# Fewer DMA issues on SyncE, a new allowance in the scheduler, and the last output tile in column halves

## The chip, the cores and the metric

The kernel runs on one core of one Trainium2 chip. The metric is the time of one execution on the device, in microseconds (us). The kernel before took 228.57 us (median of 4 runs, 227.63 to 229.99). A profile shows one execution, its span from the first to the last instruction.

## The reference, cut to what matters

```python
xn = layernorm(x)                                   # x: 2048 x 512
kv = shift_conv(k, shift_k) * v
y  = irfft(rfft(pad(kv)) * rfft(pad(ssm_k)))[:S]    # long convolution, length 4096
s  = xn * (y + kv * ssm_D)
g  = silu(w_down @ (gelu(xn @ w_gate) * (xn @ w_up)))   # 512 -> 1792 -> 512
return x + s * g
```

The Fourier transforms are done as matmuls in two stages each, with the data written to HBM and read back between the stages (ZH, ZK, ZS, ZI), because that rearranges it. The feed-forward part is TensorE's filler: plain matmuls that wait for nothing late.

## The kernel before

A small scheduler inside the program orders some hundreds of tasks before anything is built: each has an engine, an estimated duration and a priority, and the order in which it picks them becomes the fixed program of each engine. Each engine then goes through its own program in that order, with semaphore waits. So a matmul that stands too early in TensorE's program stops everything behind it: the first one that reads BK did so for 3.52 us.

```python
# scheduler: earliest start of a task after its dependency d
base = max(base, d.end + d.lat + (self.HEDGE if d.nbytes and t.opts[0][0] == "PE" else self.SEM))   # HEDGE = 1500 ns
...
# one quarter of XN transposed into xnT: four DMAs on SyncE
for j in range(4):
    S.add([("SP", 350.0)], f_transpose(j), ...)
...
# filter spectrum n read back, rows 0..127 and the two halves swapped: three DMAs
dma(e, HS[:, j, 0, :, :], ZS[n], ...)
for h in range(2):
    dma(e, HS[64 * h:64 * h + 64, j, 1, :, :], ZS[n, 64 - 64 * h:128 - 64 * h], ...)
...
# inverse result stored
S.add([("SP", 350.0)], st, r=[bo], w=[bZ["I"][n]], prio=0, nbytes=262144)
...
# end, for each pair of tiles
G = (tanh + 1) * psum ; XN = y_psum * XN ; G = G * XN ; G = G + X ; write out (256 KB)
```

Names used below: BH and BK are the inputs of the second stage for the filter and for the data; HB is the product of the two spectra (VectorE); BO is the inverse's result, copied from PSUM by ScalarE into one of two buffers and stored as ZI; BI reads it back. HS is a filter spectrum, read back from ZS; xnT is XN transposed.

## Time and profile before

| | before |
|---|---|
| median time | 228.57 us |
| profiled execution | 231.43 us, span 229.6 us |
| TensorE busy | 209.8 us (91%) |
| first matmul of real work, end of TensorE | 14.82, 224.33 us |
| after TensorE's end | 5.3 us |

In profile lines PE is TensorE (PEld its weight loads), DVE VectorE, ACT ScalarE and POOL GpSimd; SPq and ACTq are DMAs issued by SyncE and ScalarE; "out<-in" names what is written and what is read. A clock of 1.00 is TensorE at full speed, and psall is PSUM, where TensorE's results stand.

The prediction shows where TensorE waits. Here is the end of the program, on ScalarE and VectorE (start, duration, instruction, in brackets the idle time before it and what ended it):

```profile
224.35 0.60 ACT L1055 ACTIVATE G<-psall 128x512 bf16<-128x512 f32 x1 [1.56 <-PE psall L575]
224.98 0.69 DVE L1057 SCALAR_TENSOR_TENSOR G<-G,psall 128x512 bf16<-128x512 bf16 x1 [1.47 <-ACT G L1055]
225.71 0.69 DVE L1101 TENSOR_TENSOR G<-G,XN 128x1024 bf16<-128x1024 bf16 x1
226.43 0.69 DVE L1103 TENSOR_TENSOR G<-G,X 128x1024 bf16<-128x1024 bf16 x1
```

Four dependent steps follow the last matmul, then the write of two tiles.

### The profile page before, as it was taken

What the parts mean: (1) busy time and instruction counts of PE and PEld (TensorE: products, weight loads), DVE (VectorE), ACT (ScalarE), POOL (GpSimd) and SP (SyncE); (2) the same over time, 40 slices, a digit from 0 to 9 for tenths busy, and PEclk for the clock granted to TensorE, in tenths of its full rate; (3) what the DMA queues carried; (4) which work ended last, traced back from release to release, by engine and by line L of the source; (5) the groups of instructions that cost most, each with busy time, mean ns of one, the idle gap of its engine ahead of it and who ended that gap; (6) DMA issues with size and microseconds to landing.
All of it is one profiled execution on the core that took longest, in us unless ns stands there. A gap on an engine that the chain in (4) does not pass through costs nothing.

```text
span 229.6 us, 2869 instructions
## 1 busy us (share of the span) xinstructions
PE 209.8 (91%) x970; PEld 94.6 (41%) x988; DVE 169.3 (74%) x252; ACT 118.6 (52%) x151; POOL 17.5 (8%) x42
## 2 busy tenths in 40 slices
PE   7788999999959999999939999969899999999990
PEld 2553444444414444444413444424344444444440
DVE  5995799689973989892228599869677447999543
ACT  4498886767726977993620553442464332133121
POOL 8634000013000000001000000000000000000000
PEclk9999999999997999999985999999999999999998
DMA  6999999989798688789788999999951277712311
GB/s 192 385 348 359 392 373 390 416 328 189 172 320 272 237 254 275 260 283 328 196 264 283 246 285 277 325 304 316 299 189 60 91 240 254 240 46 93 141 46 46
DMA packets 47759, 57.48 MB, mean 250 GB/s; under 512 B 13824, under 2 KB 32001, under 8 KB 47744
## 3 DMA queue, kind: packets, MB, share of 16 engines
q1 hardware_dynamic: 44864, 51.00, 70.6%
q10 hardware_dynamic: 2880, 6.29, 8.1%
q8 instruction: 8, 0.13, 0.2%
q14 instruction: 7, 0.06, 0.1%
HBM read 35.78 MB, written 18.87 MB: 238 GB/s over the span
## 4 chain that ended last, share of the span: by engine, by line
PE 35%; issue 22%; SPq 18%; DMA 16%; DVE 4%; ACT 2%; POOL 1%; POOLq 0%; ACTq 0%
PE psall L575 35%; SPq L552 16%; DMA ZI<-BO 8%; DMA X<-in_A_q_dram 6%; DMA BK<-ZK 2%; SPq L773 2%; ACT BO L571 1%; DVE XN L761 1%; DVE stats L749 1%; POOL mv L758 1%; DVE HT L1040 1%; POOLq L381 0%; DVE G L1101 0%; DVE G L1057 0%; DVE G L1103 0%
## 5 line engine op out<-in xcount | busy, mean ns | idle before, releaser
L575 PE MATMUL psall<-xnT,Wg 128*128 128x512 bf16 x224 | 56.5, 389 | 0.7 <-ACT BO L571 0.4
L575 PE MATMUL psall<-xnT,Wu 128*128 128x512 bf16 x224 | 56.3, 384 | 0.1
L1037 ACT ACTIVATE GE<-psall 128x512 bf16<-128x512 f32 x56 | 33.0, 597 | 44.8 <-PE psall L575 43.5
L575 PE MATMUL psall<-Wd,HT 128*128 128x512 bf16 x219 | 51.3, 379 | 0.2
L1040 DVE TENSOR_TENSOR HT<-psall,GE 128x512 bf16<-128x512 f32 x56 | 37.6, 685 | 14.0 <-PE psall L575 12.2
L1003 DVE TENSOR_TENSOR HB<-psall,HS 128x1024 bf16<-128x1024 f32 x32 | 37.1, 1218 | 14.2 <-PE psall L575 14.2
L575 PEld LDWEIGHTS psall<-xnT,Wg 128*128 128x128 bf16 x224 | 22.2, 100 | 29.3 <-issue 3.1
L575 PEld LDWEIGHTS psall<-xnT,Wu 128*128 128x128 bf16 x224 | 22.0, 99 | 27.8 <-issue 1.6
L575 PEld LDWEIGHTS psall<-Wd,HT 128*128 128x128 bf16 x224 | 22.0, 98 | 26.4
L571 ACT ACTIVATE BO<-psall 128x1024 bf16<-128x1024 f32 x16 | 16.4, 1024 | 22.0 <-DMA ZI<-BO 12.3
L1057 DVE SCALAR_TENSOR_TENSOR G<-G,psall 128x512 bf16<-128x512 bf16 x16 | 10.7, 684 | 18.6 <-ACT G L1055 18.6
L1055 ACT ACTIVATE G<-psall 128x512 bf16<-128x512 f32 x16 | 9.3, 598 | 19.3 <-PE psall L575 19.2
L571 ACT ACTIVATE ASH<-psall 128x1024 bf16<-128x1024 f32 x16 | 16.3, 1021 | 2.7 <-PE psall L575 2.3
L575 PE MATMUL psall<-HB,MT 128*128 128x512 bf16 x61 | 15.8, 379 | 0.8 <-ACT BO L571 0.6
L938 DVE TENSOR_TENSOR KAC<-KAC,KTM 128x2048 bf16<-128x2048 bf16 x12 | 14.6, 1220 | 0.2
L936 DVE TENSOR_TENSOR KTM<-KK,SKB 128x2048 bf16<-128x2048 bf16 x12 | 14.6, 1217 | 0.1
L575 PE MATMUL psall<-BK,MT 128*128 128x512 bf16 x30 | 9.3, 412 | 5.2 <-DMA BK<-ZK 3.5
L749 DVE BATCH_NORM_STATS2 stats<-X 128x6 f32<-128x512 bf16 x16 | 10.4, 675 | 4.3 <-DMA X<-in_A_q_dram 4.3
L965 ACT ACTIVATE AST<-psall 128x1024 bf16<-128x1024 f32 x11 | 11.1, 1025 | 2.6 <-PE psall L575 2.6
L575 PE MATMUL psall<-BH,MT 128*128 128x512 bf16 x30 | 9.5, 408 | 2.8 <-DVE KTM L936 2.0
L758 POOL TENSOR_TENSOR mv<-mv,NHALF 128x4 f32<-128x4 f32 (+1 forms) x5 | 5.4, 1084 | 78.9 <-DVE mv L757 78.9
L1090 DVE TENSOR_TENSOR XN<-psall,XN 128x1024 bf16<-128x1024 f32 x8 | 9.6, 1216 | 0.7 <-PE psall L575 0.7
(69 smaller groups left out, 157.5 us busy)
## 6 DMA issues: line engine op xcount, KB each, us to landing
ZH<-ASH ACTq DMA_DIRECT2D x16, 256.0 KB, 5.8
BH<-ZH SPq DMA_DIRECT2D x16, 256.0 KB, 3.7
HS<-ZS SPq DMA_DIRECT2D x16, 256.0 KB, 5.7
HS<-ZS SPq DMA_DIRECT2D x32, 128.0 KB, 5.1
BK<-ZK SPq DMA_DIRECT2D x16, 256.0 KB, 5.6
ZI<-BO SPq DMA_DIRECT2D x16, 256.0 KB, 4.5
BI<-ZI SPq DMA_DIRECT2D x16, 256.0 KB, 4.3
ZS<-AST SPq DMA_DIRECT2D x11, 256.0 KB, 3.3
```

The source lines that it names most:

```text
L552: trk.dma(eng, lambda e: e.dma_start(out=out_ap, in_=in_ap), sem, r=r, w=w)
L571: return h.activation(o, i, ACTF.Copy)
L575: return h.matmul(o, lhsT=l, rhs=r, start=st, stop=sp)
L749: op([("DVE", 670.0)], lambda e, h, t=t: h.bn_stats(stats[:, t, :], X[:, t, :]), r=[bX[q][t % 4 // 2]], w=[bst[t]], rr=[R_X[t]], ww=[R_st[ ...
L936: op([("DVE", dur)], lambda e, h, j=j, m=m: h.tensor_tensor(KTM[:, m.slot, :, :], kk(j), sk(j), ALU.mult), r=need + [bSKB, a], w=[m], rr=l ...
L938: op([("DVE", dur)], lambda e, h, m=m: h.tensor_tensor(KAC[:, a.slot, :, :], KAC[:, a.slot, :, :], KTM[:, m.slot, :, :], ALU.add), r=[m], ...
L965: op([("ACT", act(1024))], lambda e, h, p=p, a=a: h.activation(ast["K"][a.slot].rearrange("p c d -> p (c d)"), ps(psl(p)), ACTF.Copy, scal ...
L1003: op([("DVE", dve(1024, 1))], lambda e, h, k=k, pk=pk, qq=qq, hs=hs: h.tensor_tensor(HB[:, qq.slot, :, :].rearrange("p c d -> p (c d)"), p ...
L1037: op([("ACT", act(512))], lambda e, h: h.activation(GE[:, g.slot, :], bank(pg), ACTF.Gelu_apprx_tanh), r=[pg], w=[g], rr=lambda: R_bank(pg ...
L1040: op([("DVE", dve(512, 1))], lambda e, h: h.tensor_tensor(HT[:, q % 2, m, :], bank(pu), GE[:, g.slot, :], ALU.mult), r=[pu, g], w=[bHT[q][m]],
L1057: op([("DVE", dve(512, 1))], lambda e, h, t=t, p=p: h.scalar_tensor_tensor(out=G[:, t, :], in0=G[:, t, :], scalar=1.0, in1=bank(p), op0=AL ...
L1090: op([("DVE", dve(1024, 1))], lambda e, h, p=p, xs=xs: h.tensor_tensor(xs, ps(psl(p)), xs, ALU.mult), r=[p], w=[bS[j], bXN[2 * j], bXN[2 * ...
```

## The change

The intent: relieve SyncE's in-order queue, let TensorE meet its DMA inputs later, and shorten the end. The core of the diff:

```diff
-    HEDGE = 1500.0
+    HEDGE = 3000.0          # 1000 for the first loads
...
-                for j in range(4):                      # four transposes per quarter
-                    ... in_=XN[:, 4 * q + j, :], transpose=True
-                    S.add([("SP", 350.0)], f, ...)
+                ... in_=XN[:, 4*q:4*q+4, :].rearrange("p t d -> p (t d)"), transpose=True
+                S.add([("SP", 2600.0)], f, ...)         # one, with a longer estimate
...
+                dma(e, ZS[n, 128:192], ast["K"][a.slot][0:64], ...)   # first half stored twice
-                three reads of HS
+                src = bass.AP(ZS, n * 192 * 2 * DM, [[2 * DM, 128], [128 * DM, 2], [1, 2 * DM]])
+                dma(e, HS[:, hs.slot], src, ...)                      # one read
...
-            S.add([("SP", 350.0)], ... BK read ..., prio=0.4)
+            S.add([("SP", ISSUE)], ... BK read ..., prio=-0.5)        # ISSUE = 470
-            S.add([("SP", 350.0)], st, ... ZI store ...)
+            S.add([("ACT", 350.0)], st, ... ZI store ..., lat=STORE)
-        one 1 MB transpose F1 -> G1, after stage 1
+        four of 256 KB, after the ninth inverse
...
+                cols = [(0, DM)] if t < NT - 1 else [(0, DM // 2), (DM // 2, DM)]
+                for c0, c1 in cols:
+                    g, rg = G[:, t, c0:c1], [R_G[t]]                  # region of the whole tile
+                    tanh -> g ; u = psum * XN ; g = (g + 1) * u ; g = g + x ; write out
```

Beside these, the second half of the first X load is issued by ScalarE, for the first six pairs of tiles G is multiplied by XN ahead of the inverse's last stage, and some of the scheduler's estimates change (470 ns instead of 350 for most DMA issues of SyncE, 800 instead of 1450 for one step of GpSimd).

More of the change, by code (lines that the diff above doesn't have):

```diff
@@ L27 @@
 STORE = 5000.0
+ISSUE = 470.0
 NC_PAIRS = 3
@@ L318, in run @@
                 for d in t.deps:
-                    base = max(base, d.end + d.lat + (self.HEDGE if d.nbytes and t.opts[0][0] == "PE" else self.SEM))
+                    base = max(base, d.end + d.lat + (self.SEM if not d.nbytes or t.opts[0][0] != "PE" else 1000.0 if d.eng.startswith("loads") else self.HEDGE))
                 ok = True
@@ L455, in build_kernel @@
         ZK = nc.dram_tensor("ZK", [NG, 128, DM], BF16, kind="Internal")
-        ZS = nc.dram_tensor("ZS", [NG // 2, 128, 2, DM], BF16, kind="Internal")
+        ZS = nc.dram_tensor("ZS", [NG // 2, 192, 2, DM], BF16, kind="Internal")
         ZI = nc.dram_tensor("ZI", [NG, 128, DM], BF16, kind="Internal")
@@ L523, in build_kernel @@
         R_BK = [res(f"BK{j}", BK[:, j, :, :]) for j in range(6)]
-        R_HS = [[res(f"HS{j}_0", HS[:, j, 0, :, :])] + [res(f"HS{j}_1{h}", HS[64 * h:64 * h + 64, j, 1, :, :]) for h in range(2)] for j in range(4)]
+        R_HS = [res(f"HS{j}", HS[:, j, :, :, :]) for j in range(4)]
         R_HB = [res(f"HB{j}", HB[:, j, :, :]) for j in range(6)]
@@ L530, in build_kernel @@
                "S": [trk.free_res(f"ZS{t}") for t in range(16)],
+               "D": [trk.free_res(f"ZD{t}") for t in range(16)],
                "I": [trk.free_res(f"ZI{t}") for t in range(16)]}
@@ L583, in build_kernel @@
         bmv = [[B(f"mv{q}_{h}") for h in range(2)] for q in range(NQ)]
-        bxnT = [[B(f"xnT{q}_{h}") for h in range(4 if q else 2)] for q in range(NQ)]
+        bxnT = [[B(f"xnT{q}_{h}") for h in range(1 if q else 2)] for q in range(NQ)]
         bF1, bG1, bMT, bid, bSKB = [B(f"F1_{i}") for i in range(4)], [B(f"G1_{i}") for i in range(4)], B("MT"), B("id"), B("SKB")
@@ L596, in build_kernel @@
         bG = [B(f"G{j}") for j in range(8)]
+        bGX = [B(f"GX{j}") for j in range(6)]
         bconst, bIO, bCC, bSKR = B("const"), [B(f"IO{i}") for i in range(4)], B("CC"), B("SKR")
@@ L706, in load_x @@
                 for h in range(2):
-                    load(f"x{q}_{h}", X[:, 2 * h:2 * h + 2, :], x_dr[:, 2 * h:2 * h + 2, :], R_X[2 * h:2 * h + 2], [bX[0][h]], 262144)
+                    load(f"x{q}_{h}", X[:, 2 * h:2 * h + 2, :], x_dr[:, 2 * h:2 * h + 2, :], R_X[2 * h:2 * h + 2], [bX[0][h]], 262144, ("SP", "ACT")[h])
         def load_w(i):
@@ L757, in ln @@
                 op([("DVE", 180.0)], lambda e, hd, ts=ts: hd.tensor_scalar(mv[:, ts, 2:3], mv[:, ts, 1:2], LN_EPS, None, ALU.add), r=bm, w=[be], rr=rm, ww=rm, prio=pr)
-                t_pw = op([("POOL", 1450.0)], lambda e, hd, ts=ts, n=n: hd.tensor_tensor(mv[:, ts, 3:4], mv[:, ts, 2:3], NHALF[:, 0:n, :], ALU.pow),
+                t_pw = op([("POOL", 800.0)], lambda e, hd, ts=ts, n=n: hd.tensor_tensor(mv[:, ts, 3:4], mv[:, ts, 2:3], NHALF[:, 0:n, :], ALU.pow),
                           r=[bconst, be] + bm, w=[b], rr=rm + [R_nh], ww=rm, prio=-2)
@@ L763, in ln @@
             return t_pw
-        d_xt = [dsem(f"d_xt{j}") for j in range(4)]
+        d_xt = dsem("d_xt")
         def xn_transpose(q):
@@ L769, in xn_transpose, with f @@
             if q:
-                for j in range(4):
-                    def f(e, j=j):
-                        o = xnT[:, q % 2, j, :, :]
-                        trk.dma(e, lambda h: h.dma_start(out=o, in_=XN[:, 4 * q + j, :], transpose=True), d_xt[j], r=[R_XN[4 * q + j]], w=[R_xnT[q % 2][j]])
-                    S.add([("SP", 350.0)], f, r=[bXN[4 * q + j]], w=[bxnT[q][j]], prio=-1, nbytes=131072, after=af)
+                def f(e):
+                    o = xnT[:, q % 2, :, :, :].rearrange("k j d p -> k (j d) p")
+                    trk.dma(e, lambda h: h.dma_start(out=o, in_=XN[:, 4 * q:4 * q + 4, :].rearrange("p t d -> p (t d)"), transpose=True), d_xt, r=R_XN[4 * q:4 * q + 4], w=R_xnT[q % 2])
+                S.add([("SP", 2600.0)], f, r=bXN[4 * q:4 * q + 4], w=bxnT[q], prio=-1, nbytes=524288, after=af)
                 return
@@ L790, in xn_transpose @@
                    rr=lambda p=p: R_bank(p), ww=R_xnT[q % 2][2 * hf:2 * hf + 2], prio=-1, after=af)
+        d_out = []
         gu_tasks = [[] for _ in range(NQ)]
@@ L901, in st @@
                 dma(e, dst, ast[x][a.slot], d_ast[x][a.slot], [R_AST[x][a.slot]], [R_Z[x][t]])
-            t_st = S.add([("ACT" if x == "H" else "SP", 350.0)], st, r=[a], w=[bZ[x][t]], prio=0, lat=STORE if x == "H" else 0.0, nbytes=262144 if x == "K" else 0)
+            t_st = S.add([("ACT", 350.0) if x == "H" else ("SP", ISSUE)], st, r=[a], w=[bZ[x][t]], prio=0, lat=STORE if x == "H" else 0.0, nbytes=262144 if x == "K" else 0)
             if x == "H":
@@ L957, in build_kernel @@
         d_bh = [dsem(f"d_bh{j}") for j in range(4)]
+        d_dup = [dsem(f"d_dup{j}") for j in range(5)]
         h2_tasks = []
@@ L961, in h_stage2 @@
             bh, p, a = B(f"bh{n}", pBH), B(f"psf{n}", pC), B(f"hf{n}", pAST["K"])
-            S.add([("SP", 350.0)], lambda e, n=n, bh=bh: dma(e, BH[:, bh.slot, :, :], z_pair(ZH, n), d_bh[bh.slot], R_Z["H"], [R_BH[bh.slot]]),
+            S.add([("SP", ISSUE)], lambda e, n=n, bh=bh: dma(e, BH[:, bh.slot, :, :], z_pair(ZH, n), d_bh[bh.slot], R_Z["H"], [R_BH[bh.slot]]),
                   r=bZ["H"], w=[bh], prio=0.5, nbytes=262144, after=zh_tasks)
@@ L966, in h_stage2, with st @@
                r=[p], w=[a], rr=lambda p=p: R_ps[psl(p)], ww=lambda a=a: [R_AST["K"][a.slot]], prio=2.5, after=kshift_tasks[:1])
-            S.add([("SP", 350.0)], lambda e, n=n, a=a: dma(e, ZS[n], ast["K"][a.slot], d_ast["K"][a.slot], [R_AST["K"][a.slot]], [R_Z["S"][n]]),
-                  r=[a], w=[bZ["S"][n]], prio=0, nbytes=262144)
+            def st(e, n=n, a=a):
+                dma(e, ZS[n, 0:128], ast["K"][a.slot], d_ast["K"][a.slot], [R_AST["K"][a.slot]], [R_Z["S"][n]])
+                dma(e, ZS[n, 128:192], ast["K"][a.slot][0:64], d_dup[a.slot], [R_AST["K"][a.slot]], [R_Z["D"][n]])
+            S.add([("SP", 950.0)], st, r=[a], w=[bZ["S"][n]], prio=0, nbytes=393216)
         for n in range(16):
@@ L974, in build_kernel @@
             stage1("K", t, V[:, t, :], R_V[t], [bKV[t // 4]], ZK, 3)
-        d_g1 = dsem("d_g1")
-        S.add([("SP", 350.0)], lambda e: trk.dma(e, lambda h: h.dma_start(out=G1[:].rearrange("k t c p -> k (t c) p"), in_=F1[:].rearrange("p t c k -> p (t c k)"), transpose=True),
-                                                d_g1, r=R_F1, w=R_G1), r=bF1, w=bG1, prio=8, nbytes=1048576, after=s1_tasks["K"])
         d_bk = [dsem(f"d_bk{j}") for j in range(6)]
-        d_hs = [[dsem(f"d_hs{j}_{h}") for h in range(3)] for j in range(4)]
+        d_hs = [dsem(f"d_hs{j}") for j in range(4)]
         d_bo = [dsem(f"d_bo{j}") for j in range(2)]
@@ L991, in ld_s @@
             def ld_s(e, n=n, hs=hs):
-                j = hs.slot
-                dma(e, HS[:, j, 0, :, :], ZS[n], d_hs[j][0], [R_Z["S"][n]], [R_HS[j][0]])
-                for h in range(2):
-                    dma(e, HS[64 * h:64 * h + 64, j, 1, :, :], ZS[n, 64 - 64 * h:128 - 64 * h], d_hs[j][1 + h], [R_Z["S"][n]], [R_HS[j][1 + h]])
-            S.add([("SP", 1000.0)], ld_s, r=[bZ["S"][n]], w=[hs], prio=0.5, nbytes=524288, after=kshift_tasks)
-            S.add([("SP", 350.0)], lambda e, n=n, bk=bk: dma(e, BK[:, bk.slot, :, :], z_pair(ZK, n), d_bk[bk.slot], R_Z["K"], [R_BK[bk.slot]]),
-                  r=bZ["K"], w=[bk], prio=0.4, nbytes=262144)
+                src = bass.AP(ZS, n * 192 * 2 * DM, [[2 * DM, 128], [128 * DM, 2], [1, 2 * DM]])
+                dma(e, HS[:, hs.slot, :, :, :].rearrange("p k c d -> p k (c d)"), src, d_hs[hs.slot], [R_Z["S"][n], R_Z["D"][n]], [R_HS[hs.slot]])
+            S.add([("SP", ISSUE)], ld_s, r=[bZ["S"][n]], w=[hs], prio=0.5, nbytes=524288, after=kshift_tasks)
+            S.add([("SP", ISSUE)], lambda e, n=n, bk=bk: dma(e, BK[:, bk.slot, :, :], z_pair(ZK, n), d_bk[bk.slot], R_Z["K"], [R_BK[bk.slot]]),
+                  r=bZ["K"], w=[bk], prio=-0.5, nbytes=262144)
             S.add([("PE", pe(2))], fwd(pk, BK, R_BK, bk), r=[bMT, bk], w=[pk], prio=3.5, lat=200.0, after=t_inv[n - 2:n - 1] if n >= 2 else [])
@@ L1004, in build_kernel @@
                     HB[:, qq.slot, :, :].rearrange("p c d -> p (c d)"), ps(psl(pk)), HS[:, hs.slot, k, :, :].rearrange("p c d -> p (c d)"), ALU.mult),
-                   r=[pk, hs], w=[qq], rr=lambda k=k, pk=pk, hs=hs: R_ps[psl(pk)] + (R_HS[hs.slot][1:] if k else R_HS[hs.slot][:1]), ww=lambda qq=qq: [R_HB[qq.slot]], prio=0.9)
+                   r=[pk, hs], w=[qq], rr=lambda k=k, pk=pk, hs=hs: R_ps[psl(pk)] + [R_HS[hs.slot]], ww=lambda qq=qq: [R_HB[qq.slot]], prio=0.9)
             def inv(e, pi=pi, q1=q1, q2=q2):
@@ L1013, in build_kernel @@
             t_inv.append(S.add([("PE", pe(4))], inv, r=[bMT, q1, q2], w=[pi], prio=3, lat=200.0))
-            op([("ACT", act(1024)), ("DVE", dve(1024, 1))], lambda e, h, pi=pi, bo=bo: copy(e, h, BO[:, bo.slot, :, :].rearrange("p c d -> p (c d)"), ps(psl(pi))),
+            op([("ACT", act(1024))], lambda e, h, pi=pi, bo=bo: copy(e, h, BO[:, bo.slot, :, :].rearrange("p c d -> p (c d)"), ps(psl(pi))),
                r=[pi], w=[bo], rr=lambda pi=pi: R_ps[psl(pi)], ww=lambda bo=bo: [R_BO[bo.slot]], prio=0.9)
@@ L1018, in st, with g1 @@
                 dma(e, bass.AP(ZI, 2 * n * 128 * DM, [[DM, 128], [128 * DM, 2], [1, DM]]), BO[:, bo.slot, :, :], d_bo[bo.slot], [R_BO[bo.slot]], [R_Z["I"][n]])
-            S.add([("SP", 350.0)], st, r=[bo], w=[bZ["I"][n]], prio=0, nbytes=262144)
+            S.add([("ACT", 350.0)], st, r=[bo], w=[bZ["I"][n]], prio=0.8, lat=STORE)
+        d_g1 = [dsem(f"d_g1{i}") for i in range(4)]
+        for i in range(4):
+            def g1(e, i=i):
+                ts = slice(4 * i, 4 * i + 4)
+                trk.dma(e, lambda h: h.dma_start(out=G1[:, ts].rearrange("k t c p -> k (t c) p"), in_=F1[:, ts].rearrange("p t c k -> p (t c k)"), transpose=True),
+                        d_g1[i], r=R_F1[ts], w=R_G1[ts])
+            S.add([("SP", 1350.0)], g1, r=[bF1[i]], w=[bG1[i]], prio=8, nbytes=262144, after=[t_inv[8]])
         def unit(q, m):
@@ L1044, in down @@
             for jt in range(4):
-                p = B(f"psd{q}_{jt}", pF)
                 t = 4 * q + jt
-                for m0, m1 in ((0, 4), (4, 9), (9, 14)):
-                    def f(e, p=p, jt=jt, m0=m0, m1=m1):
-                        for m in range(m0, m1):
-                            trk.op("PE", lambda h, m=m: mm(h, bank(p), HT[:, q % 2, m, 128 * jt:128 * (jt + 1)], Wd[:, m, :], m == 0, m == MF - 1),
-                                   r=[R_HT[q % 2][m], R_Wd[m // 7]], w=R_bank(p), accum=True)
-                    down_tasks[q].append(S.add([("PE", pe(m1 - m0))], f, r=(bHT[q] if jt else bHT[q][m0:m1]) + bWd[m0 // 7:(m1 + 6) // 7], w=[p], prio=9 + q - 0.5 if jt or m1 == MF else 10.05 + q, lat=200.0))
@@ L1054, in down @@
-                bt = B(f"tanh{q}_{jt}")
-                op([("ACT", act(512))], lambda e, h, t=t, p=p: h.activation(G[:, t, :], bank(p), ACTF.Tanh, scale=0.5), r=[p], w=[bt],
-                   rr=lambda p=p: R_bank(p), ww=[R_G[t]], prio=1, after=zh_tasks + (h2_tasks if q >= 2 else []))
-                op([("DVE", dve(512, 1))], lambda e, h, t=t, p=p: h.scalar_tensor_tensor(out=G[:, t, :], in0=G[:, t, :], scalar=1.0, in1=bank(p), op0=ALU.add, op1=ALU.mult),
-                   r=[p, bt], w=[bG[t // 2]], rr=lambda p=p, t=t: R_bank(p) + [R_G[t]], ww=[R_G[t]], prio=1)
+                cols = [(0, DM)] if t < NT - 1 else [(0, DM // 2), (DM // 2, DM)]
@@ new lines, in down, with pc, f @@
+                for c0, c1 in cols:
+                    p = B(f"psd{q}_{jt}_{c0}", pF)
+                    def pc(p=p, c0=c0, c1=c1):
+                        return bank(p)[:, c0:c1]
+                    for m0, m1 in ((0, 4), (4, 9), (9, 14)):
+                        def f(e, p=p, jt=jt, m0=m0, m1=m1, pc=pc, c0=c0, c1=c1):
+                            for m in range(m0, m1):
+                                trk.op("PE", lambda h, m=m: mm(h, pc(), HT[:, q % 2, m, 128 * jt:128 * (jt + 1)], Wd[:, m, c0:c1], m == 0, m == MF - 1),
+                                       r=[R_HT[q % 2][m], R_Wd[m // 7]], w=R_bank(p), accum=True)
+                        down_tasks[q].append(S.add([("PE", pe(m1 - m0, c1 - c0))], f, r=(bHT[q] if jt else bHT[q][m0:m1]) + bWd[m0 // 7:(m1 + 6) // 7],
+                                                   w=[p], prio=9 + q - 0.5 if jt or m1 == MF else 10.05 + q, lat=200.0))
+                    n = c1 - c0
+                    g, rg = G[:, t, c0:c1], [R_G[t]]
+                    bt = B(f"tanh{q}_{jt}")
+                    op([("ACT", act(n))], lambda e, h, g=g, pc=pc: h.activation(g, pc(), ACTF.Tanh, scale=0.5), r=[p], w=[bt],
+                       rr=lambda p=p: R_bank(p), ww=rg, prio=1, after=zh_tasks + (h2_tasks if q >= 2 else []))
+                    if q < NQ - 1:
+                        op([("DVE", dve(512, 1))], lambda e, h, g=g, pc=pc: h.scalar_tensor_tensor(out=g, in0=g, scalar=1.0, in1=pc(), op0=ALU.add, op1=ALU.mult),
+                           r=[p, bt], w=[bG[t // 2]], rr=lambda p=p, rg=rg: R_bank(p) + rg, ww=rg, prio=1)
+                        continue
+                    u, x = XN[:, t, c0:c1], X[:, t, c0:c1]
+                    bu, b2 = B(f"u{t}_{c0}"), B(f"o{t}_{c0}")
+                    op([("DVE", dve(n, 1))], lambda e, h, u=u, pc=pc: h.tensor_tensor(u, pc(), u, ALU.mult), r=[p, bS[t // 2]], w=[bu],
+                       rr=lambda p=p, t=t: R_bank(p) + [R_XN[t]], ww=[R_XN[t]], prio=0.8)
+                    op([("DVE", dve(n, 1))], lambda e, h, g=g, u=u: h.scalar_tensor_tensor(out=g, in0=g, scalar=1.0, in1=u, op0=ALU.add, op1=ALU.mult),
+                       r=[bu, bt], w=[b2], rr=rg + [R_XN[t]], ww=rg, prio=1)
+                    op([("DVE", dve(n, 2))], lambda e, h, g=g, x=x: h.tensor_tensor(g, g, x, ALU.add), r=[b2], w=[b2], rr=rg + [R_X[t]], ww=rg, prio=1)
+                    R_o, d_o = trk.free_res(f"outl{t}_{c0}"), dsem(f"d_outl{t}_{c0}")
+                    d_out.append(d_o)
+                    S.add([("SP", ISSUE)], lambda e, t=t, c0=c0, c1=c1, g=g, rg=rg, R_o=R_o, d_o=d_o: dma(e, out_dr[:, t, c0:c1], g, d_o, rg, [R_o]),
+                          r=[b2], w=[B(f"outl{t}")], prio=1, nbytes=256 * n)
@@ L1065, in build_kernel @@
                 unit(q, m)
-            down(q)
+            if q < NQ - 1:
+                down(q)
         d_bi = [dsem(f"d_bi{j}") for j in range(8)]
@@ L1079, in ld @@
                     dma(e, BI[:, bi.slot, :, :], src, d_bi[bi.slot], R_Z["I"], [R_BI[bi.slot]])
-                S.add([("SP", 350.0)], ld, r=bZ["I"], w=[bi], prio=0.5, nbytes=262144)
+                S.add([("SP", ISSUE)], ld, r=bZ["I"], w=[bi], prio=0.5, nbytes=262144)
             def y(e, j=j, bis=bis, p=p):
@@ L1088, in build_kernel @@
             S.add([("PE", pe(4))], y, r=[bG1[j // 2]] + bis, w=[p], prio=3, lat=200.0)
-            xs = XN[:, 2 * j:2 * j + 2, :].rearrange("p t d -> p (t d)")
-            op([("DVE", dve(1024, 1))], lambda e, h, p=p, xs=xs: h.tensor_tensor(xs, ps(psl(p)), xs, ALU.mult), r=[p], w=[bS[j], bXN[2 * j], bXN[2 * j + 1]],
-               rr=lambda p=p, j=j: R_ps[psl(p)] + R_XN[2 * j:2 * j + 2], ww=R_XN[2 * j:2 * j + 2], prio=3)
-        d_out = [dsem(f"d_out{j}") for j in range(8)]
-        for j in range(8):
+            ts = slice(2 * j, 2 * j + 2)
@@ new lines, in build_kernel @@
+            xs, g = (T[:, ts, :].rearrange("p t d -> p (t d)") for T in (XN, G))
+            if j < 6:
+                op([("DVE", dve(1024, 2))], lambda e, h, g=g, xs=xs: h.tensor_tensor(g, g, xs, ALU.mult), r=[bG[j], *bXN[ts]], w=[bGX[j]],
+                   rr=R_G[ts] + R_XN[ts], ww=R_G[ts], prio=4)
+            else:
+                g = xs
+            R_g = R_G[ts] if j < 6 else R_XN[ts]
+            op([("DVE", dve(1024, 1))], lambda e, h, p=p, g=g: h.tensor_tensor(g, ps(psl(p)), g, ALU.mult), r=[p, *([bGX[j]] if j < 6 else [])], w=[bS[j], *([] if j < 6 else bXN[ts])],
+               rr=lambda p=p, R_g=R_g: R_ps[psl(p)] + R_g, ww=R_g, prio=3)
@@ L1096, in build_kernel @@
+        down(NQ - 1)
+        for j in range(6):
+            d_out.append(dsem(f"d_out{j}"))
             g = G[:, 2 * j:2 * j + 2, :].rearrange("p t d -> p (t d)")
-            xs = XN[:, 2 * j:2 * j + 2, :].rearrange("p t d -> p (t d)")
             x = X[:, 2 * j:2 * j + 2, :].rearrange("p t d -> p (t d)")
-            rg, rx, rxn = R_G[2 * j:2 * j + 2], R_X[2 * j:2 * j + 2], R_XN[2 * j:2 * j + 2]
-            b1, b2 = B(f"sg{j}"), B(f"o{j}")
-            op([("DVE", dve(1024, 2))], lambda e, h, g=g, xs=xs: h.tensor_tensor(g, g, xs, ALU.mult), r=[bG[j], bS[j]], w=[b1],
-               rr=rg + rxn, ww=rg, prio=4)
@@ L1103, in build_kernel @@
-            op([("DVE", dve(1024, 2))], lambda e, h, g=g, x=x: h.tensor_tensor(g, g, x, ALU.add), r=[b1], w=[b2], rr=rg + rx, ww=rg, prio=4)
-            S.add([("SP", 350.0)], lambda e, j=j, rg=rg: dma(e, out_dr[:, 2 * j:2 * j + 2, :], G[:, 2 * j:2 * j + 2, :], d_out[j], rg, [R_out[j]]),
+            rg, rx = R_G[2 * j:2 * j + 2], R_X[2 * j:2 * j + 2]
+            b2 = B(f"o{j}")
+            op([("DVE", dve(1024, 2))], lambda e, h, g=g, x=x: h.tensor_tensor(g, g, x, ALU.add), r=[bS[j]], w=[b2], rr=rg + rx, ww=rg, prio=3.5)
@@ L1105, in build_kernel @@
+            S.add([("SP", ISSUE)], lambda e, j=j, rg=rg, d_o=d_out[-1]: dma(e, out_dr[:, 2 * j:2 * j + 2, :], G[:, 2 * j:2 * j + 2, :], d_o, rg, [R_out[j]]),
                   r=[b2], w=[B(f"out{j}")], prio=4, nbytes=262144)
```

## The prediction

> **What bounds the kernel now.** I read the busy table first, then the slices, the timeline of TensorE, windows around its gaps, the waits, and SyncE's own timeline.
>
> ```profile
> span 229.6 us, 2869 instructions
> PE 209.8 (91%) x970; PEld 94.6 (41%) x988; DVE 169.3 (74%) x252; ACT 118.6 (52%) x151; POOL 17.5 (8%) x42
> ```
>
> TensorE is the bound. Both kernels issue 908 matmuls' worth of 512 columns. Warm, one follows the other by 0.216 us (the last 50 start at 213.15 and follow each other to 223.95). Its first matmul of real work starts at 14.82, so 896 x 0.216 = 193.5 us would end at 208.4; it ends at 224.33. So 15.9 us are lost in between, and 5.3 us follow as a tail. These lines of the TensorE timeline show most of the loss:
>
> ```profile
> 67.01 0.38 PE L575 MATMUL psall<-BH,MT 128*128 128x512 bf16 x1 [2.04 <-DVE KTM L936]
> 68.11 1.01 PE L575 MATMUL psall<-BH,MT 128*128 128x512 bf16 x2 [0.72 <-DMA BH<-ZH]
> ...
> 120.42 1.01 PE L575 MATMUL psall<-BK,MT 128*128 128x512 bf16 x2 [3.52 <-DMA BK<-ZK]
> ...
> 154.50 0.61 PE L575 MATMUL psall<-BK,MT 128*128 128x512 bf16 x2 [1.62 <-ACT BO L571]
> ```
>
> The number in brackets is idle time before the row. The cost of each is read from windows (columns: stretch, its length, busy time and count per engine, granted clock, DMA share, GB/s):
>
> ```profile
> 64.80:71.40 6.60, 3.83 (x10) 1.29 (x11) 3.08 (x4) 2.58 (x3) 0.00 (x0) 0.74 0.91 274
> 116.90:126.60 9.70, 6.18 (x18) 2.22 (x18) 5.16 (x6) 1.19 (x2) 0.00 (x0) 0.65 0.83 282
> 149.60:163.30 13.70, 11.02 (x49) 4.38 (x49) 9.21 (x11) 5.56 (x7) 0.00 (x0) 1.00 1.07 311
> ```
>
> Window A did 10 matmuls (2.2 us of work) in 6.6: **4.4 us lost**. B did 18 (3.9) in 9.7: **5.8 lost**. C did 49 (10.6) in 13.7: **3.1 lost**. Sum 13.3 of the 15.9. In A and B much of it is lost after the wait, at a lower clock.
>
> Why those waits: SyncE's timeline. Before A it spends 50.31 to 61.40 issuing eight transposes; the first BH read goes out at 63.30. Before B four transposes take 105.92 to 111.08, six HS reads 3.3 us more, and the first BK read goes out at 115.25 and lands at 120.3:
>
> ```profile
> 105.92 5.16 SPq L773 DMA_TRANSPOSE xnT<-XN  x4
> 111.13 0.57 SPq L552 DMA_DIRECT2D ZK<-ASX  x1
> 111.76 3.32 SPq L552 DMA_DIRECT2D HS<-ZS  x6
> 115.25 0.97 SPq L552 DMA_DIRECT2D BK<-ZK  x2
> ```
>
> In C ScalarE waits for a free BO buffer ("ACT BO L571 <- DMA ZI<-BO: 12.3, 6" in the waits): the ZI store stands behind HS reads in SyncE's program, and holds PSUM that TensorE needs.
>
> **What the Trainium skill says.** (1) "TensorE: Matmul & The Clock Gate", Part 1, section "What's actually happening": the array falls to half rate after an idle window of about 3.4 us. The trace agrees: the slice 120 to 125, after 3.52 us of idling, has a clock of 0.50. A wait removed is thus worth more than its idle time. (2) "DMA: Bandwidth & Descriptors", "Rules for kernel authors": spreading DMAs over issuing engines brings no bandwidth, only issue time. In window C the DMA share is 1.07 at 311 GB/s, so stores by ScalarE free SyncE, not the DMA engines. (3) "PSUM — Partial Sum Buffer", "PSUM bank collisions raise a hardware error": two engines must not touch one bank at once. The kernel's tracker obeys, which orders ScalarE and VectorE in the new tail; no run here shows a collision.
>
> **The change part by part**, with the instruction order of the built kernel beside the old one.
>
> *Start.* The second X load goes to ScalarE's queue, and VectorE does one table phase (0.68 + 0.43 us) less before the last XN; the transposes on TensorE stay. First real matmul about 14.3 instead of 14.8: -0.5 us.
>
> *Window A.* One transpose per quarter. The 1 MB transpose of G held SyncE 5.09 us, so I take 2.6 for 512 KB, my estimate. The second waits for the first and for XN (last written 56.4): it ends near 59, three ZK stores follow (1.5), BH goes out near 60.5 and lands 3.7 later, near 64.5. The scheduler, with a larger allowance for DMA, now puts 252 instead of 236 matmuls ahead of BH: 3.5 us later, near 67.8. Margin 3 us: A goes, -4.4.
>
> *Window B.* 474 instead of 456 matmuls stand ahead of the first BK (+3.9 us of cover), and BK comes straight after one transpose, with the HS reads ahead of it. The transpose cannot start before the last XN, near 106 (VectorE, 105.99 before); BK goes out near 108.8, lands 5.0 later (as before) at 113.8; TensorE asks for it near 115.7. Margin 2 us: B goes, -5.8.
>
> *Window C.* HS is one read (0.47 us of issue) instead of three (1.6), 16 x 1.1 = 18 us less on SyncE. ZI leaves right after BO on ScalarE (16 x 0.35 us; ScalarE is 52% busy). So the wait behind other issues goes. But the bytes stay, and the duplicate half of ZS adds 16 x 128 KB = 2.1 MB of writing. From 108.8 to about 165 must move: BK 4.2, HS 6.3 (12 left), ZI 3.4, late ZS with duplicates 2.0, BH 0.3, G transpose 1.0: 17.2 MB, at 311 GB/s 55 us of a window of 56. VectorE has 32 HB at 1.216 (38.9) plus about 10 of 0.685 and some G work: near 49 of 52 us. Both are full, so I keep 2.5 of the 3.1 us.
>
> *Tail.* Before: 224.33 to 229.6: tanh 0.61, three VectorE steps of 0.70, then the output write (landing 2.1). The last tile is now two column halves; the work after PSUM is shorter, but both halves are tracked as ONE region of G and of XN. In the order's wait list, the last add waits for the output write of the first half, and the first half's add waits for the second half's tanh. From T, TensorE's end, with 256-column steps taken from 512 and 1024 columns (0.42 PSUM or two-step, 0.28 bf16 add, 0.38 tanh): VectorE is behind with tile 14 and starts the second product near T+0.6; tanh follows it to T+1.45; first add to 1.75; its write lands at 3.9; last add to 4.2; last write lands at 6.3, end 6.6. Against 5.3: **+1.3 us**, where the halves were meant to save about 1.5. The 14 extra matmul starts (28 of 256 columns) cost no columns.
>
> Moving G times XN ahead of the inverse puts 6 x 0.68 us of VectorE work earlier: beside other work.
>
> Sum: 229.6 - 0.5 - 4.4 - 5.8 - 0.6 + 1.3 = 219.6 of span; I add 0.1 for small waits, 219.7. The median of the runs before lies 1.2 under the profiled span (228.39 against 229.6), so **218.5 us**.
>
> **Rivals.** (i) *DMA becomes the bound in the inverse stage.* For it: 17.2 MB in 56 us at a share above 1.0, and transposes move slower (240 GB/s in 125 to 130). Against: HS has four buffers and reads run ahead. If HB arrives late by half a microsecond per spectrum, TensorE loses 5 to 8 us more: 222 to 225. (ii) *B only moves.* The BK reads still wait for every ZK store and for XN of the last quarter; if VectorE reaches XN 3 us later, the wait and the half clock return, +3 to 5: 222 to 223. (iii) *All waits go and the tail is as designed*, if the false waits overlap what I think they don't: 219.7 - 2.5 - 2.8 of span, about 213. (iv) *Nothing gained, slower*: would need the duplicate stores to stop SyncE in the BH stage; SyncE has idle gaps of a microsecond between most issues there, so unlikely.
>
> **Range and chances.** Middle 218.5; (iii) sets the low end, 213.5, (i) and (ii) the high end, 225. The 2% line is 223.8; only (i) or (ii) in full, or both in part, get there. Faster 0.86, same 0.12, slower 0.02.
>
> **What would show it.** First matmul of real work near 14.3. No TensorE idle above 0.5 us before BH and BK near 67 and 116, clock 1.00 there. Fewer waits of BO for ZI; DMA share still above 1.0 from 125 to 160, remaining waits in that stretch on HS or BO. TensorE ends near 213; after it some 6.6 us with an idle gap of about 2 us on VectorE before the last add, ended by the output write. Wrong would be: a gap above 2 us before BK, a clock of 0.5 after it, or a tail under 5 us.

## The result

The changed kernel takes **220.25 us** (median of 4 runs, 219.99 to 221.08), 0.9637 of the time before, 95% interval 0.958 to 0.9694. A ratio here is the mean time of one kernel's fast runs over that of the other's of the same rounds, so not quite the ratio of the medians. All of these runs and both profiles are recorded as fast. The profiled execution of the kernel before, at 231.43 us, is however 1.7% above the fastest of the four runs beside it (227.63); so differences between the two profiles are larger than those of the times.

The page of the changed kernel begins so:

```profile
span 218.5 us, 2888 instructions
PE 205.5 (94%) x1002; PEld 95.6 (44%) x1002; DVE 172.6 (79%) x259; ACT 119.3 (55%) x152; POOL 17.5 (8%) x42
```

TensorE works for a larger share of a shorter span. Its timeline at the places where it used to wait:

```profile
68.28 1.03 PE L577 MATMUL psall<-BH,MT 128*128 128x512 bf16 x4
...
116.20 0.59 PE L577 MATMUL psall<-BK,MT 128*128 128x512 bf16 x2
...
140.50 1.04 PE L577 MATMUL psall<-xnT,Wu 128*128 128x512 bf16 x4 [0.84 <-ACT BO L573]
...
146.82 0.61 PE L577 MATMUL psall<-BK,MT 128*128 128x512 bf16 x2 [0.54 <-ACT BO L573]
```

No bracket stands behind the first BH and BK: no wait of over 0.1 us is left there. Of the inverse's waits, 0.84 and 0.54 us remain (and 0.25 for a late BH at 127.83). The windows around the three places (length, then busy time and count of TensorE, weight loads, VectorE, ScalarE, GpSimd, then clock, DMA share, GB/s):

```profile
64.80:71.40 6.60, 6.60 (x32) 3.04 (x31) 6.44 (x9) 3.68 (x6) 0.00 (x0) 1.00 0.58 173
112.00:121.00 9.00, 9.00 (x44) 4.04 (x42) 6.68 (x8) 3.40 (x6) 0.00 (x0) 1.00 1.02 323
136.00:160.00 24.00, 22.62 (x104) 9.86 (x103) 18.47 (x19) 10.46 (x14) 0.00 (x0) 1.00 1.05 319
```

The first stretch, 6.6 us long in both kernels, did 32 matmuls where it had done 10, at full clock. In the inverse stage the DMA engines are still full (share 1.05). And SyncE, ahead of BK:

```profile
107.27 4.65 SPq L775 DMA_TRANSPOSE xnT<-XN  x1
112.11 3.02 SPq L554 DMA_DIRECT2D BK<-ZK  x6
```

This single transpose of a quarter holds SyncE 4.65 us, hardly less than the four did (5.16); the two others, before BH, held it 3.24 and 2.02 us. BK goes out at 112.11, 3.1 us earlier than before, and lands 3.0 us later (5.0 before), at 115.1; TensorE now asks for it at 116.20.

The end of the program, after TensorE's last matmul (212.26):

```profile
212.75 0.42 DVE L1082 TENSOR_TENSOR XN<-psall,XN 128x256 bf16<-128x256 f32 x1
213.21 0.38 ACT L1073 ACTIVATE G<-psall 128x256 bf16<-128x256 f32 x1 [1.63 <-DVE XN L1082]
213.62 0.29 DVE L1086 TENSOR_TENSOR G<-G,X 128x256 bf16<-128x256 bf16 x1 [0.45 <-ACT G L1073]
213.95 0.43 DVE L1084 SCALAR_TENSOR_TENSOR G<-G,XN 128x256 bf16<-128x256 bf16 x1
216.01 0.29 DVE L1086 TENSOR_TENSOR G<-G,X 128x256 bf16<-128x256 bf16 x1 [1.63 <-DMA out_dram<-G]
```

The last add stands idle for 1.63 us until the first half's *output write* has landed: this tail takes 218.5 - 212.26 = 6.2 us, against 5.3 before.

### The profile page after: what moved, and what is told of

Read it like the earlier page. It is cut to its first block, busy times and chain, and to the rows that moved or that the text cites. A ratio compares the mean times of both kernels' runs of the same rounds, so it can differ in the third digit from the quotient of the medians.

```text
span 218.5 us, 2888 instructions
## 1 busy us (share of the span) xinstructions
PE 205.5 (94%) x1002; PEld 95.6 (44%) x1002; DVE 172.6 (79%) x259; ACT 119.3 (55%) x152; POOL 17.5 (8%) x42
## 4 chain that ended last, share of the span: by engine, by line
PE 61%; DMA 16%; SPq 15%; DVE 4%; ACT 2%; issue 1%; ACTq 0%
PE psall L577 61%; SPq L554 15%; DMA X<-in_A_q_dram 7%; DMA ZI<-BO 6%; DMA BH<-ZH 3%; ACT BO L573 1%; DVE stats L752 1%; DMA out_dram<-G 1%; DVE G L1084 1%; DVE XN L1082 1%; DVE XN L764 1%; DVE V L943 1%; ACT G L1073 0%; DVE G L1086 0%; DVE mv L753 0%
## 5 line engine op out<-in xcount | busy, mean ns | idle before, releaser
L577 PE MATMUL psall<-xnT,Wu 128*128 128x512 bf16 x224 | 55.5, 379 | 1.0 <-ACT BO L573 0.8
L577 PE MATMUL psall<-xnT,Wg 128*128 128x512 bf16 x224 | 53.9, 379 | 0.0
L577 PE MATMUL psall<-Wd,HT 128*128 128x512 bf16 (+1 forms) x238 | 52.3, 367 | 0.6 <-DVE HT L1050 0.6
L577 PEld LDWEIGHTS psall<-Wd,HT 128*128 128x128 bf16 x238 | 23.1, 98 | 26.2 <-DVE HT L1050 1.3
L1073 ACT ACTIVATE G<-psall 128x512 bf16<-128x512 f32 (+1 forms) x17 | 9.5, 576 | 20.5 <-PE psall L577 18.8
L577 PE MATMUL psall<-HB,MT 128*128 128x512 bf16 x64 | 16.4, 379 | 0.0
L969 ACT ACTIVATE AST<-psall 128x1024 bf16<-128x1024 f32 x11 | 11.0, 1023 | 3.8 <-PE psall L577 3.8
L1076 DVE SCALAR_TENSOR_TENSOR G<-G,psall 128x512 bf16<-128x512 bf16 x12 | 7.9, 683 | 2.9 <-ACT G L1073 2.7
L573 ACT ACTIVATE AST<-psall 128x1024 bf16<-128x1024 f32 x9 | 9.2, 1029 | 1.6 <-PE psall L577 1.6
L577 PE MATMUL psall<-HTr,F 128*128 128x512 bf16 x32 | 9.2, 380 | 0.8 <-ACT GE L1047 0.5
L577 PEld LDWEIGHTS psall<-HB,MT 128*128 128x128 bf16 x64 | 6.2, 98 | 7.7 <-DVE HB L1004 0.4
```

Source lines behind the costliest of these rows:

```text
L573: return h.activation(o, i, ACTF.Copy)
L577: return h.matmul(o, lhsT=l, rhs=r, start=st, stop=sp)
L969: op([("ACT", act(1024))], lambda e, h, p=p, a=a: h.activation(ast["K"][a.slot].rearrange("p c d -> p (c d)"), ps(psl(p)), ACTF.Copy, scal ...
L1073: op([("ACT", act(n))], lambda e, h, g=g, pc=pc: h.activation(g, pc(), ACTF.Tanh, scale=0.5), r=[p], w=[bt], rr=lambda p=p: R_bank(p), ww= ...
L1076: op([("DVE", dve(512, 1))], lambda e, h, g=g, pc=pc: h.scalar_tensor_tensor(out=g, in0=g, scalar=1.0, in1=pc(), op0=ALU.add, op1=ALU.mult ...
```

## The experiments

Twelve kernels were run (E5 and E11 are the changed kernel again), all correct, on three chips, one chip for each group of four. The time before was 229.72, 231.92 and 231.03 us there, so runs of different groups are compared by their ratio to before at most, and small differences only within a group. (The changed kernel itself had ratios of 0.9637, 0.948 and 0.959 in its three groups of rounds.) A run is slow when it is over 1.5% above the fastest of the same kernel; the others are fast. Medians are of all runs, ratios of fast runs alone; E2, E5, E10 and E12 had one slow run each. Where an experiment "keeps the order", the scheduler was given the same tasks with the same estimates, and only what a task issues was changed: the programs of TensorE and VectorE were the same instruction for instruction. Counts of matmuls ahead of BH or BK are taken from the built programs, and count those of 512 columns.

My theory after the first look: the waits before BH and BK went because TensorE meets them later *and* SyncE reaches them earlier. The rivals: one of the two alone does it.

### E1: the halves as regions of their own

```diff
+                    if len(cols) > 1:
+                        rg, rxn = [res(..., G[:, t, c0:c1])], [res(..., XN[:, t, c0:c1])]
```

> The changed kernel with one edit: the two column halves of the last tile are tracked as regions of their own. My theory (the last add waits for the output write of the first half, 213.95 to 216.01 on VectorE): everything up to the end of TensorE stays, the wait of the last add on the output write is gone, the tail after TensorE falls from 6.2 us to about 4.2, so about 2.0 us off: 218.2 us. Rival (that wait lies beside another write that ends as late anyway, or VectorE is simply late): the time stays at 220.

Measured: 219.27 us, 0.9552 of before (0.9483 to 0.962). The last steps now run without waiting for the write:

```profile
213.77 0.38 ACT L1076 ACTIVATE G<-psall 128x256 bf16<-128x256 f32 x1 [1.50 <-DVE XN L1085]
214.19 0.42 DVE L1087 SCALAR_TENSOR_TENSOR G<-G,XN 128x256 bf16<-128x256 bf16 x1 [0.25 <-ACT G L1076]
214.65 0.29 DVE L1089 TENSOR_TENSOR G<-G,X 128x256 bf16<-128x256 bf16 x1
```

TensorE ended at 212.93 and the span at 217.2: a tail of 4.3 us. The wait on the write was real, and needless: the two halves share no byte. This group has no run of the changed kernel, so the gain is read from the profiles here; E12 has it in the times.

### E2: the last tile whole

```diff
-                cols = [(0, DM)] if t < NT - 1 else [(0, DM // 2), (DM // 2, DM)]
+                cols = [(0, DM)]
```

> The changed kernel with the last tile whole again (one output write of 128 KB), the rest as changed. My theory: the halves as shipped cost time; whole, the tail is tanh 0.60, product 0.69, second step 0.69, add 0.42 and a write of about 2, some 4.6 us instead of 6.2: about 1.6 us off, 218.6 us. Rival (halves save time as intended): about 1 us slower than the changed kernel, 221.

Measured: 219.74 us, 0.956 of before (0.9457 to 0.9663), with a tail of 218.1 - 213.17 = 4.9 us. So the halves as shipped cost 1.3 us of tail against no halves at all, and with regions of their own they save 0.6 us by the profiles. In the times E1 and E2 cannot be told apart, and neither can be told from the changed kernel, which ran on another chip.

### E3 and E4: the allowance alone, taken away and put in

```diff
# E3, in the changed kernel; E4 is the reverse, in the kernel before
-    HEDGE = 3000.0   (1000 for the first loads)
+    HEDGE = 1500.0
```

> The changed kernel with the scheduler's old allowance for DMA (1500 instead of 3000, no exception for the first loads), so TensorE meets BH and BK earlier in its program; all the DMA issues stay fewer. Theory that the later placement in TensorE's program removes the waits: the waits before BH or BK come back in part, 3 to 6 us slower than the changed kernel, 223 to 226. Rival that the relief of SyncE alone removes them: within 1 us of 220.

> The kernel before with only the new allowance (3000), none of the fewer issues. Theory that the later placement does most of it: 3 to 6 us faster than before, 222.5 to 225.5, with the waits before BH and BK gone or halved and the wait for BO still there. Rival that SyncE's relief does it: within 1.5 us of before, 227 to 230, waits unchanged.

Measured: E3 222.75 us, 0.9696 of before (0.9621 to 0.977). E4 226.9 us, 0.9895 (0.9811 to 0.9979). E4 gained about 2.4 us, clear of zero, but under 2% and between the 3 us of one theory and the 1.5 of the other: the waits before BK shrank from 3.52 to 2.19 us (1.86 and 0.33), those before BH from 2.76 to 1.24, and a wait of 2.60 us for BO appeared at 133.14. E3 lies between its two expectations; its interval overlaps that of the changed kernel, measured on another chip, so what taking the allowance away costs is not shown by the times. Its waits were 1.58 us before BK and 1.96 us in the feed-forward part.

Neither is a clean test of TensorE's place alone, for the allowance reorders SyncE's program too. In E3 the first BK no longer follows the transpose directly: six ZS stores, a ZK store and two HS reads stand between, and it goes out only at 118.09. It has even *more* matmuls ahead of it than in the changed kernel (488 against 474; 456 before, 468 in E4), and still they do not cover it. My reading, not tested, is that the longer estimates for DMA issues push BK back by themselves. So the allowance alone brings part of the gain; what it is worth within the changed kernel stays open.

### E5 to E8: one saving of issues undone at a time, the order kept

E5 is the changed kernel again. E6 reads HS in three pieces and stores no duplicate; E7 transposes a quarter with four DMAs; E8 lets SyncE issue the ZI stores:

```diff
# E6
-  dma(e, ZS[n, 128:192], ...)  ;  one read of HS
+  three reads of HS
# E7
-  one transpose of XN[:, 4q:4q+4, :]
+  for j in range(4): transpose of XN[:, 4q+j, :]
# E8
-  dma(e, ... ZI ...)           # e is ScalarE
+  dma("SP", ... ZI ...)
```

> The changed kernel itself, on the chip of the next three runs, as their yardstick. All theories: 0.96 of the time of before, 220 to 221.5 us; losses of TensorE in the inverse stage 1.5 to 3 us, none before BH and BK over 0.5 us.

> The changed kernel, every engine's order kept, with the filter spectrum read in three pieces again and without the duplicate half in HBM (32 more reads issued, 16 stores and 2.1 MB fewer). Theory that SyncE's issue time of these reads was no limit once ZI is off its queue (SyncE waits for XN before the last transpose anyway): within 1 us of the changed kernel, either way. Rival that these reads delay BK and HS: 2 to 3 us slower, with waits before BK and HB.

> The changed kernel, every engine's order kept, with each quarter transposed by four transposes again. The one of the last quarter took 4.65 us of SyncE in the changed kernel, four took 5.16 before, so theory: BK goes out some 0.5 us later, where TensorE has no margin: 0 to 1 us slower than the changed kernel. Rival (the single transpose is what removed the waits before BH and BK): 3 us or more slower, with waits before both.

> The changed kernel, every engine's order of work kept, with the inverse's stores issued by SyncE again, at the place that the schedule gives them. Theory that the store stood behind reads that wait: waits of BO for ZI come back (12 us in total, 3 us of it on TensorE before BK and HB), 1.5 to 4 us slower than the changed kernel. Rival (the stage is bound by DMA bytes, who issues is the same): within 0.7 us.

| | median us | of before | 95% interval |
|---|---|---|---|
| E5 changed | 220.85 | 0.948 | 0.9396 to 0.9565 |
| E6 three reads | 221.59 | 0.9527 | 0.9451 to 0.9604 |
| E7 four transposes | 221.22 | 0.9531 | 0.9452 to 0.961 |
| E8 ZI by SyncE | 220.36 | 0.9489 | 0.9423 to 0.9554 |

None of the three is worth anything that these runs can show. By the ratios E6 and E7 are 1.1 and 1.2 us slower than E5, and the interval of each ratio reaches nearly 2 us to either side: the times neither confirm nor refute my theory (within 1 us), but in the profiles TensorE waits for no read of BH or BK, as it would have by the rivals. E8 did not go as I expected: I said 1.5 to 4 us slower, and it was as fast as E5. BO's waits for ZI, the last number of each line, do not separate the two either. The lines are of E8, of E5, and of E11, which is the changed kernel once more:

```profile
L573 ACT ACTIVATE BO<-psall 128x1024 bf16<-128x1024 f32 x16 | 16.4, 1023 | 19.0 <-DMA ZI<-BO 12.9
L573 ACT ACTIVATE BO<-psall 128x1024 bf16<-128x1024 f32 x16 | 16.4, 1024 | 16.8 <-DMA ZI<-BO 10.2
L573 ACT ACTIVATE BO<-psall 128x1024 bf16<-128x1024 f32 x16 | 16.4, 1023 | 18.8 <-DMA ZI<-BO 12.9
```

The DMA engines are full in this stage (share 1.05 in the changed kernel), which fits; who issues the store made no difference that shows. Each saving could still be hidden by the slack that the other two leave, so the next group undid all three at once.

### E9 to E11: order and issues, crossed

E9 is E6, E7 and E8 together: the new order with the old issues. E10 puts the three savings into the kernel before and keeps its order of TensorE and VectorE. E11 is the changed kernel, as yardstick.

```diff
# E10, in the kernel before, the scheduler's estimates untouched
+  duplicate half of ZS, one read of HS
+  the fourth of each quarter's transpose tasks issues one DMA for all four
+  dma("ACT", ... ZI ...)
```

> The changed kernel with every engine's order of work kept, and all three savings of DMA issues undone together: filter spectra read in three pieces and no duplicate half, four transposes per quarter, inverse stores by SyncE. Theory A (the new order of the programs carries the gain, the number of issues does not): within 1.5 us of the changed kernel, about 0.955 of before. Theory B (the issues carry it; undone one by one each was hidden by the slack that the other two left): 4 us or more slower than the changed kernel, with waits before BK and HB, 0.97 or more of before.

> The kernel before with TensorE's and VectorE's order kept word for word, and the three savings of issues put in (one read per filter spectrum with the duplicate half, one transpose per quarter, inverse stores by ScalarE). Theory A (order): within 2 us of before, waits before BH and BK still there. Theory B (issues): 4 us or more faster than before, waits before BH and BK gone.

> The changed kernel again, as the yardstick on the chip of the three other runs: 0.95 to 0.965 of before, by all theories.

Measured, all in the same rounds (median us, ratio to before, 95% interval; whether E10 gains 2% is unclear, that it gains is not):

| | old issues | new issues |
|---|---|---|
| old order | 231.03, 1 | E10: 225.98, 0.9772 (0.972 to 0.9824) |
| new order | E9: 221.84, 0.9611 (0.9572 to 0.9651) | E11: 221.34, 0.959 (0.9554 to 0.9627) |

This settles the main question, order against number of issues. The new order with the old issues has nearly all of the gain: 9.0 us of 9.5, if the ratios are multiplied by 231.03. The issues alone bring 5.3 us. The two do not add up: once the order is new, the fewer issues bring 0.5 us, within the intervals. E9's SyncE shows why:

```profile
50.39 10.56 SPq L776 DMA_TRANSPOSE xnT<-XN  x8
...
63.36 6.59 SPq L554 DMA_DIRECT2D BH<-ZH  x6
...
107.72 5.16 SPq L776 DMA_TRANSPOSE xnT<-XN  x4
113.05 3.02 SPq L554 DMA_DIRECT2D BK<-ZK  x6
```

BH goes out at 63.36, as late as before the change (63.30). And yet TensorE does not wait:

```profile
68.44 1.03 PE L577 MATMUL psall<-BH,MT 128*128 128x512 bf16 x4
...
116.36 0.59 PE L577 MATMUL psall<-BK,MT 128*128 128x512 bf16 x2
```

It has 16 more matmuls of other work ahead of BH (3.5 us), and BH landed at 66.6. The issues are as many as before; the place in TensorE's program is later. For BK the order acts on both sides: 18 more matmuls stand ahead of it in TensorE's program, and in SyncE's program no HS read stands between the transpose and BK any more, so BK goes out 2.2 us earlier than before. In E10 the waits are shorter than before but there:

```profile
67.38 0.59 PE L576 MATMUL psall<-BH,MT 128*128 128x512 bf16 x2 [1.71 <-DMA BH<-ZH]
...
116.94 0.59 PE L576 MATMUL psall<-BK,MT 128*128 128x512 bf16 x2 [1.85 <-DMA BK<-ZK]
...
133.59 1.04 PE L576 MATMUL psall<-BK,MT 128*128 128x512 bf16 x4 [2.68 <-ACT BO L572]
```

So fewer issues alone remove neither wait. In time E10 goes with theory B (5.3 us, where B said 4 or more and A under 2), in its waits with A, though they are shorter. One reason is the clock: in the slices with the waits of 1.71 and 1.85 us it stayed at 1.00, so only the waits themselves are lost, where before the waits around BH and BK (2.76 and 3.52 us) cost 4.4 and 5.8 us by the windows, the rest of it at a lower clock. After the third wait, 2.68 us, the clock was 0.51 from 135 to 137.

"Order" here is all that E9 keeps: the estimates, the allowance, the priority of BK, the moved transposes of G, and the new end of the program. E4 shows what the allowance does without the rest; which of the others weighs most stays open.

### E12: the best version

The changed kernel with the regions of E1, and the last half's tanh ahead of its product.

> The changed kernel with the halves of the last tile as regions of their own, and the last half's tanh placed ahead of its product (TensorE's order the same). Theory: tail after TensorE about 4.0 us instead of 6.2, so 2.0 to 2.3 us faster than the changed kernel of the same rounds, about 0.99 of it. Rival (the write of the first half ends as late in any case): the same time.

Measured: **218.86 us**, 0.9469 of before (0.9422 to 0.9516). Against E11 of the same rounds that is 0.9469 / 0.959 = 0.987, 2.8 us less (2.5 by the medians, which contain a slow run), and the intervals do not overlap. It beats both kernels. I expected 2.0 to 2.3 us; what the swap of the last two steps adds to the regions was not separated.

## Why the prediction was right

The time (220.25 against 218.5) lies in the range, and the kernel is faster by clearly over 2%. By its steps:

- **What bounds the kernel, and the three stretches.** Right. The waits before BH and BK are gone and the clock is full there. In the inverse stage I kept 2.5 us of loss; the three profiles of the changed kernel show idle time of 1.6, 2.1 and 3.9 us (E5 and E11 are the other two). The DMA share there was 1.04, but VectorE was not full as I had it: busy 44.4 of the 56.2 us from 108.8 to 165, not 49 of 52.
- **The start.** Right in direction. The first matmul of real work came at 13.90 instead of 14.82, 0.9 us where I said 0.5; the other profiles of the changed kernel have 13.83 (E5) and 14.87 (E11).
- **Window A and B, in their reasons.** Half right. I gave two reasons for each, an earlier read and a later matmul, and the sum did not need to choose. E9 shows that the later place in TensorE's program is enough for A, and that order alone, on both queues, is enough for B; E10 shows that fewer issues alone are enough for neither. For A the margin of 3 us held: BH went out at 62.13, landed at 65.3, and TensorE asked for it at 68.28.
- **The transpose of a quarter, 2.6 us.** Wrong where it mattered most. The two before BH took 3.24 and 2.02 us, together what I had said; the one before BK took 4.65 (3.4 to 5.2 in the nine fast profiles with single transposes). It also began at 107.27, not near 106, because VectorE finished XN at 107.25. So BK went out at 112.11 instead of 108.8, 3.3 us late. That the wait still went is in part luck: BK landed 3.0 us after its issue, where I had taken 5.0 from the kernel before, and of the margin of 2 us that I worked out 1.1 was left.
- **ScalarE's stores.** Not shown. I said that the wait of BO behind other issues goes. BO waited for ZI 12.3 us in the kernel before, and 7.6, 10.2 and 12.9 us in three profiles of the changed kernel, so no fall shows; and with SyncE issuing again (E8) nothing was lost. This fits the rival that the DMA engines are the bound of this stage, without the 5 to 8 us that it threatened; no experiment took bytes away to test it.
- **The tail.** Right, read from the wait list alone: 6.6 us predicted, 6.2 measured, and the wait of the last add on the write, 2 us predicted, was 1.63. E1 confirmed the cause.
- **From span to time.** Wrong, and it hid another error. I took the time as 1.2 us *under* the span, because I subtracted the span of one execution from the median of others. An execution's time is 1.8 to 1.9 us *over* its own span (231.43 for 229.6 before, 220.37 for 218.5 after). The profiled execution before was simply slower than the median by 2.9 us. So the gain between the two profiles, 11.1 us, overstates the gain in the medians, 8.3 us, and my 9.9 was too much for the same reason. The predicted span, 219.7, was 1.2 us over the measured one; the two errors partly cancelled, which is luck: with 1.8 us added, as the runs show, the same span would have given 221.5.

## What to carry to other kernels

Where engines run fixed programs in order, a wait for a DMA can be shortened from either end, and the two gains need not add (9.0 and 5.3 us alone, 9.5 together): put other work ahead of the consumer, or bring the transfer forward; ask which of the two is already enough before the second is built. When a tile is split to overlap its output with the rest of the work, split its dependency tracking too, or the overlap turns into a wait, here 1.63 us for an output write. And compare spans with spans and times with times.

## What the Trainium skill lacked or had wrong

- "TensorE: Matmul & The Clock Gate", "What's actually happening", names at least one idle window of about 3.4 us for the fall to half rate. In the kernel before, waits of 2.04 and 0.72 us, ending 1.1 us apart, already brought a clock of 0.50 from 68 to 71 us (0.74 over the 6.6 us around them). Single waits of 1.62 (before), 1.71, 1.85 (E10), 2.22 (E6) and 2.61 us (E11) left it at 1.00, and single waits of 2.60 (E4) and 2.68 us (E10) were followed by 0.50 and 0.51, so the length of a wait alone did not decide it here. The 3.52 us wait, followed by 0.50 in the slice 120 to 125, agrees with the page.
- "DMA: Bandwidth & Descriptors", "Latency and other measured facts", gives 261 GB/s for a DMA transpose with a non-contiguous middle dimension, measured on one kernel, but no spread. Here the changed kernel's three transposes of 512 KB from SBUF to SBUF landed 4.3 to 6.7 us after their issue (median 6.1, some 86 GB/s by that time, which is beside other traffic and so not the same measure), and their issues held SyncE's queue for 2.02 to 4.65 us; four of 128 KB held it 5.16 us.
- The same page, "Anatomy of one DMA — SWDGE (gpsimd) path", has about 2.0 us of fixed cost for DMAs issued by GpSimd. For small writes from SyncE to HBM, another path, the changed kernel shows 1.6 us to landing (its two writes of 64 KB).
- The same page's "Rules for kernel authors" (spreading DMAs over engines saves issue time alone) held: E8, with 16 issues moved back to SyncE, was as fast, so here even the saved issue time was worth nothing that shows.
